# Order of the first loads, no held-back loads, and a new engine order in a one-core pre-norm block

## The chip, the cores and the metric

The kernel runs on one core of one Trainium2 chip. The metric is the device time of one execution in microseconds (us). Three executions of the kernel before gave 197.2, 198.14 and 198.29 us; the median is 198.14 us.

One further execution was taken by the hardware profiler. All rows of the profile in this document count their time from the first instruction of that execution.

## What is computed

The input is x of 2048 rows by 512 columns in bf16. The reference, cut to what matters:

```python
h  = x + _A_ref(_layernorm(x), A_wqkv, A_wo)
h2 = h + _B_ref(_layernorm(h), B_W_gate, B_W_up, B_W_down)

# _A_ref: 32 heads of 16; each position sees 8 positions, 2 apart
qkv = x @ wqkv
idx = pos[:, None] - (jnp.arange(8) * 2)[None, :]
logits = einsum("bhsd,bhswd->bhsw", q, k[idx]) * 16 ** -0.5   # idx < 0 masked
attn = softmax(logits)
o = einsum("bhsw,bhswd->bhsd", attn, v[idx])
return o @ wo

# _B_ref
gate, up = x @ W_gate, x @ W_up          # 512 -> 1376
return (relu(gate) * up) @ W_down        # 1376 -> 512
```

Attention reaches back 14 positions only, so it is made of elementwise products on VectorE, with small matmuls that sum over the 16 entries of a head. The large matmuls are the projections to q, k and v, the output projection, and the gated MLP.

## The kernel before

**Chunks.** The 2048 rows are four chunks of 512, and a chunk is four blocks of 128 rows. A step is named here as in the code, with the chunk behind a slash: `qkv5/1` is the sixth projection of chunk 1. The steps that matter below are these.

- `xst`, `xag` (lines 465 to 472): mean and variance of one block on DVE, from the block of x that a DMA has brought into `x_sm`. `xrl`, `xre` (491, 492): the reciprocal root on ACT, by Ln and Exp.
- `xxn` (495 to 510): the normalised block into a `row` tile, on ACT for chunks 1 and 3 (line 498, with `xnb` on DVE ahead of it), on DVE for chunks 0 and 2 (line 501).
- `xtp` with `xte` or `xtv` (523 to 548): transpose of the block on PE and its copy out of PSUM into a `quad` tile, by ACT or, for block 1 of chunk 0, by DVE at line 544. Chunk 3 has `xtd` (518 to 521) in place of it: a DMA transpose from `row` to `quad` on SP's queue, four of them.
- `qkv0` to `qkv11` (565 to 598): twelve projections of four matmuls each, q and k in turn (0 to 7), then v (8 to 11), each moved out of PSUM by ACT at line 579 (`qe`). In chunk 0 the first six are split into three parts, `qka`, `qkb`, `qkc`; `qka` needs the first two blocks of x and the first two pieces of the q, k weights alone.
- `pr0`, `pr1` (605 to 644): products of q and shifted k on DVE, for the near and the far four of the eight positions. In chunk 0 each is four half-size products (line 634); elsewhere two of full size (line 619). `sc` (625) sums them on PE, `ex` (683) is the exponential on ACT, `mk` (686) the mask of chunk 0 on DVE.
- `bd0S`, `bd1S` (741 to 747): four DMAs each on SP's queue, which spread one `ex` tile over the partitions of a `big` tile.
- `mu` (line 775, or 790 in two halves `mu..a` and `mu..c` for chunk 0): attention weights times shifted v on DVE. `ta` (818): the sum of the two halves of that product by an accumulating DMA of 512 KB, issued from POOL. `tree`, `om` (778, 782, 812): the rest of the sum on DVE, and in chunk 0 the division.
- `wo` (854, 857), `rs`, `hnm`, `hsq`, `hxn`, `htp` or `htd`: output projection, residual and second layer norm. `mm` (927, 894), `ue`, `ge`, `gu`: gate and up projections. `dn` (977), `o`, `os`: down projection, residual and store.
- `lg` (834 to 839): a copy on POOL that makes the loads of the up and down weights, `ldu` and `ldd`, wait for the last `tree` or `om` step with t = 3 of chunk 0.

**Order.** The program is not written in this order. Every step is added to a plan with its engine, a modelled duration, what it depends on and what buffers it takes. The list `RANK` at the top has one number for each step in the order of adding; each engine executes its steps in rising rank. So `RANK` fixes the sequence of PE, DVE, ACT, SP and POOL, and the engines work through it strictly in that sequence. The modelled durations and the due times `XT`, `WT` of the loads only say which of several equal buffers a step gets and how the sequences are merged into one program.

**First loads.** `setup()` (312 to 346) issues the loads of the first microseconds. SP's and ACT's queues take in turn a block of x of chunk 0 (128 KB) and a piece of the q, k weights (256 KB), lines 315 to 319. Behind them on SP's queue come the four blocks of chunk 1 (335), the v weights (337), chunks 2 and 3 of x (340), the output weights (342) and the gate weights. Three tiny copies on POOL, lines 333, 336 and 338, hold these loads back: each reads a tile that an earlier load fills and writes into the tile of the next load, so that next load waits for the earlier one to land.

**Filling.** `warm` (416 to 422) is 56 matmuls of 128 columns on a zeroed tile. `fill` (424 to 430) adds `NFILL` more behind the transposes of blocks 0 and 1.

Of the kernel before, what the change touches and what calls it, by code (L numbers as in the profile page):

```python
# [12 lines left out]
ACT = mybir.ActivationFunctionType  # L13
ALU = mybir.AluOpType
# [188 lines left out]
def kernel(  # L203
# [11 lines left out]
    nc = tc.nc  # L215
    Bsz, S, D = A_x.shape
# [3 lines left out]
    NT = D // P  # L220
# [7 lines left out]
    PRD = ()  # L228
    ODA = (0, 1)
# [9 lines left out]
    BPC = CS // P  # L239
# [72 lines left out]
    def setup():  # L312

        w3_r = A_wqkv.rearrange("(dt p) f -> p dt f", p=P)
        for i in range(2):
            for n, q in enumerate((nc.sync, nc.scalar)):
                j = 2 * i + n
                q.dma_start(x_sm[:, j:j + 1, :], x_rows[:, j:j + 1, :])
                q.dma_start(wqk_sb[:, j:j + 1, :], w3_r[:, j:j + 1, 0:2 * D])  # L319
# [13 lines left out]
        nc.gpsimd.tensor_copy(out=x_sm[0:1, BPC:2 * BPC, 0:1], in_=x_sm[0:1, 3, 0:BPC])  # L333
        for j in range(BPC, 2 * BPC):
            nc.sync.dma_start(x_sm[:, j:j + 1, :], x_rows[:, j:j + 1, :])
        nc.gpsimd.tensor_copy(out=wv_sb[0:1, 0, 0:1], in_=wqk_sb[0:1, 3, 0:1])
        nc.sync.dma_start(wv_sb[:], w3_r[:, :, 2 * D:3 * D])
        nc.gpsimd.tensor_copy(out=x_sm[0:1, 2 * BPC, 0:1], in_=x_sm[0:1, 2 * BPC - 1, 0:1])
# [35 lines left out]
    NWARM, NFILL = 56, (13, 10, 0)  # L374
    NHALF = 6
    XT = (3.55, 3.4, 6.1, 5.85, 9.0, 9.3, 9.6, 10.0, 15.2, 16.75)
    WT = (7.7, 7.7, 5.6, 12.05, 18.0, 24.95, 21.45, 28.8)
# [21 lines left out]
    MM, TP = 0.2165, 0.057  # L399
    SW = 0.21  # L400
    PEL = 0.22
    A5, A10, AX, AS = 0.485, 0.91, 0.75, 0.21
# [151 lines left out]
    for tk in range(NCK):  # L554
# [50 lines left out]
        for hf in range(2):  # L605
            sc, ex = Buf(at_s), Buf(ex_s)
            scd, prd = [], []
            for t in range(0, NT, 2):
# [13 lines left out]
                def f_sc(t=t, sc=sc, pb=pb):  # L622
                    for u in range(2):
                        for g in range(4):
                            nc.tensor.matmul(sc.t[g * HB:(g + 1) * HB, :], lhsT=sel[:],  # L625
                                             rhs=pb.t[:, 4 * u + g, :], start=(t + u == 0),
                                             stop=(t + u == NT - 1), tile_position=(0, g * HB))
# [13 lines left out]
                else:  # L641
                    a = add(("pr%d" % hf, tk), "DVE", D40, f_pr, [d[k] for k in (t, t + 1) for d in (qd, kd, kp)],
                            apr, take=[pb], use=[qT], lat=DL)
                    prd.append((a, pb, f_sc))
# [29 lines left out]
            elif tk in MERGE:  # L674
                scd = [add(("sc%d" % hf, tk), "PE", 4 * MM + SW, lambda p=prd: [f() for _, _, f in p],
# [173 lines left out]
        for j in range(BPC):  # L849
# [20 lines left out]
            if tk in RPE:  # L870
                a = add(("rs%d" % j, tk), "ACT", 0.57, f_rs, [a], base + 50, take=[sm], use=[od], lat=AL)
            else:
                a = add(("rs%d" % j, tk), "DVE", 0.63, f_rs, [a], base + 50, take=[sm], use=[od], lat=DL)
# [190 lines left out]
```

## Time and profile before

| what | value |
|---|---|
| median of three executions | 198.14 us (197.2 to 198.29) |
| span of the profiled execution | 199.0 us |
| PE busy in it | 189.6 us, 1120 matmuls |
| DVE, ACT, POOL busy | 147.9, 116.7, 17.7 us |
| mean granted TensorE clock | 0.991 |
| first projection matmul starts | 8.32 us |
| longest wait of PE | 3.06 us, ends at 37.20 us |
| last matmul ends | about 195.4 us |

How to read the rows that follow. A row of the timeline has the start, the time, the engine (PEld is the weight load of TensorE, SPq the queue that SP issues from), the line of the kernel, the operation, the tile that it writes and those that it reads, the shape, and how often in a row. Behind it, in brackets, is the time that the engine had been idle and what ended that. A row of a table of windows has the stretch, its length, the busy time of PE, PEld, DVE, ACT and POOL, then the granted TensorE clock, the busy share of the 16 DMA engines and the rate in GB/s. One operation's busy time contains some latency, so where several follow each other, the distance from start to start is what one costs.

### The profile page before, as it was taken

The numbers are of one execution on the slowest core, as the hardware profiler recorded it, in microseconds if no ns is written. First come the engines' busy times: TensorE is split into PE (matmuls) and PEld (weight loads), VectorE is DVE, ScalarE is ACT, GpSimd is POOL, SyncE is SP. The second block draws the span as 40 slices with busy tenths as digits, with TensorE's granted clock in tenths as the row PEclk, the third lists the DMA queues.
The fourth block names the chain that finished last, engine by engine and source line by source line (L and its number), as shares of the span: only waits on it lengthen the run. The fifth ranks groups of instructions, "written<-read, shape, count | busy, mean of one in ns | idle before, by whom it ended". The sixth has DMA issues, their size and how long they took to land.

```text
span 199.0 us, 3083 instructions
## 1 busy us (share of the span) xinstructions
PE 189.6 (95%) x1120; PEld 98.5 (50%) x1139; DVE 147.9 (74%) x239; ACT 116.7 (59%) x241; POOL 17.7 (9%) x35
## 2 busy tenths in 40 slices
PE   8899998599999999999999999999999999999992
PEld 8895455245445534554444445544454544455451
DVE  6889999969969999999998769999954311214322
ACT  3579999326779676775536659606458725146300
POOL 3000002520000003300024010010010010000000
PEclk9999999879999999999999999999999999999999
DMA  6889386999600535967379973360030454000303
GB/s 207 231 274 381 96 183 126 190 187 350 217 0 0 137 78 105 190 127 160 80 146 174 188 174 65 65 120 3 0 53 8 103 178 110 0 0 0 109 6 126
DMA packets 25070, 24.61 MB, mean 124 GB/s; under 512 B 11136, under 2 KB 21344, under 8 KB 25056
## 3 DMA queue, kind: packets, MB, share of 16 engines
q1 hardware_dynamic: 22032, 16.23, 29.7%
q0 software_dynamic: 2304, 7.34, 20.2%
q10 hardware_dynamic: 720, 0.85, 1.2%
q8 instruction: 9, 0.15, 0.3%
q14 instruction: 5, 0.04, 0.1%
HBM read 8.42 MB, written 2.10 MB: 53 GB/s over the span
## 4 chain that ended last, share of the span: by engine, by line
PE 90%; DMA 5%; ACT 1%; issue 1%; DVE 1%; ACTq 0%
PE bank L927 34%; PE bank L571 20%; PE bank L977 19%; PE bank L854 7%; PE bank L625 4%; PE bank L894 3%; DMA quad<-row 3%; DMA x_sm<-in_A_x_dram 2%; PE bank L530 1%; ACT quad L579 1%; PE bank L857 0%; PE bank L700 0%; DVE st L466 0%; ACT lnd L706 0%; ACTq L319 0%
## 5 line engine op out<-in xcount | busy, mean ns | idle before, releaser
L927 PE MATMUL bank<-quad,wgu_sb 128*128 128x512 bf16 x311 | 72.0, 379 | 0.4
L927 PEld LDWEIGHTS <-wgu_sb 128*128 128x128 bf16 x320 | 31.0, 98 | 36.5 <-issue 0.8
L977 PE MATMUL bank<-wd_sb,gT 128*128 128x512 bf16 (+2 forms) x185 | 40.4, 367 | 0.2
L571 PE MATMUL bank<-quad,wqk_sb 128*128 128x512 bf16 (+1 forms) x149 | 31.2, 358 | 3.5 <-DMA quad<-row 3.1
L931 ACT CAST up_sb<-bank 128x512 bf16<-128x512 f32 x40 | 22.8, 589 | 19.5 <-PE bank L927 15.9
L934 ACT ACTIVATE gr<-bank 128x512 bf16<-128x512 f32 x40 | 23.3, 601 | 17.6 <-PE bank L927 10.9
L619 DVE TENSOR_TENSOR big<-quad,kT 128x4096 bf16<-128x4096 bf16 x12 | 27.2, 2284 | 2.4 <-ACT quad L579 2.2
L977 PEld LDWEIGHTS <-gT 128*128 128x128 bf16 (+1 forms) x187 | 18.1, 98 | 19.7 <-issue 0.4
L775 DVE TENSOR_TENSOR big<-big,vT 128x4096 bf16<-128x4096 bf16 x12 | 27.1, 2284 | 0.4 <-issue 0.2
L571 PEld LDWEIGHTS <-wqk_sb 128*128 128x128 bf16 x152 | 17.0, 115 | 15.1 <-issue 6.0
L955 DVE TENSOR_TENSOR gT<-gr,up_sb 128x1024 bf16<-128x1024 bf16 x20 | 13.7, 686 | 12.4 <-ACT up_sb L931 7.9
L990 DVE TENSOR_TENSOR row<-x_sm,bank 128x512 bf16<-128x512 bf16 (+1 forms) x9 | 5.5, 625 | 17.0 <-PE bank L977 17.0
L818 POOL DMA_DIRECT2D big<-big x12 | 10.5, 872 | 85.4 <-DVE big L775 59.8
L778 DVE TENSOR_TENSOR big<-big 128x1024 bf16<-128x1024 bf16 (+2 forms) x24 | 16.7, 728 | 0.8 <-DMA big<-big 0.8
L571 PE MATMUL bank<-quad,wv_sb 128*128 128x512 bf16 x61 | 15.7, 380 | 0.3 <-issue 0.2
L854 PE MATMUL bank<-wo_sb,quad 128*128 128x512 bf16 x62 | 14.9, 379 | 0.1
L579 ACT CAST vT<-bank 128x512 bf16<-128x512 f32 x16 | 9.0, 603 | 7.4 <-PE bank L571 7.4
L455 ACT ACTIVATE row<-x_sm,mv 128x512 bf16<-128x512 bf16 x12 | 8.5, 713 | 5.4 <-DVE mv L447 5.3
L466 DVE BATCH_NORM_STATS2 st<-x_sm 128x6 f32<-128x512 bf16 x16 | 10.3, 675 | 0.8 <-DMA x_sm<-in_A_x_dram 0.8
L546 ACT COPY quad<-bank 128x1024 bf16<-128x1024 bf16 (+1 forms) x10 | 8.5, 890 | 4.0 <-PE bank L530 4.0
L501 DVE TENSOR_SCALAR row<-x_sm,mv,rs 128x512 bf16<-128x512 bf16 x24 | 8.9, 406 | 2.5 <-ACT rs L483 2.5
L579 ACT CAST quad<-bank 128x512 bf16<-128x512 f32 x16 | 9.3, 593 | 2.3 <-PE bank L571 2.1
(77 smaller groups left out, 167.0 us busy)
## 6 DMA issues: line engine op xcount, KB each, us to landing
big<-big POOLq DMA_DIRECT2D x12, 512.0 KB, 5.4
big<-ex SPq DMA_DIRECT2D x32, 128.0 KB, 3.1
wgu_sb<-in_B_W_gate_dram SPq DMA_DIRECT2D x2, 688.0 KB, 9.2
wgu_sb<-in_B_W_up_dram SPq DMA_DIRECT2D x2, 688.0 KB, 6.0
wd_sb<-in_B_W_down_dram SPq DMA_DIRECT2D x2, 640.0 KB, 8.2
x_sm<-in_A_x_dram SPq DMA_DIRECT2D x2, 512.0 KB, 6.5
x_sm<-up_sb POOLq DMA_DIRECT2D x4, 256.0 KB, 3.4
out_dram<-x_sm SPq DMA_DIRECT2D x4, 256.0 KB, 3.1
```

Of the source, the lines that this page charges most:

```text
L571: nc.tensor.matmul(mm.t[:, lo:hi], lhsT=wv_sb[:, dt, t:D:NT] if c == 2 else wqk_sb[:, dt, c * D + t:(c + 1) * D:NT], rhs=xnT.t[:, dt, lo:h ...
L579: nc.scalar.copy(out=o, in_=mm.t[:])
L619: V.tensor_tensor(out=pb.t[:].rearrange("p (t w) s -> p t w s", t=2), in0=q4, in1=k4, op=ALU.mult)
L775: V.tensor_tensor(out=mt.t[:], in0=ab.t[:], in1=v8, op=ALU.mult)
L778: V.tensor_tensor(out=mt.t[:, 0:n, :], in0=mt.t[:, 0:n, :], in1=mt.t[:, n:2 * n, :], op=ALU.add)
L818: nc.gpsimd.dma_start(mt.t[:, 0:4, :], mt.t[:, 4:8, :], accum_op=ALU.add)
L854: nc.tensor.matmul(od.t[:], lhsT=OT.t[:, t, j * P:(j + 1) * P], rhs=wo_sb[:, t, :], start=(t == 0), stop=(t == NT - 1 and tk not in RPE))
L927: nc.tensor.matmul(mm.t[:fs, lo:hi], lhsT=wgu_sb[:, dt, g, ft * P: ft * P + fs], rhs=hnT.t[:, dt, lo:hi], start=(dt == 0), stop=(dt == NT ...
L931: nc.scalar.copy(out=ub.t[:fs, i, :], in_=um.t[:fs, :])
L934: nc.scalar.activation(out=gr.t[:fs, i, :], in_=gm.t[:fs, :], func=ACT.Relu)
L955: V.tensor_tensor(out=gt.t[:fs, 0:n, :], in0=gr.t[:fs, 0:n, :], in1=ub.t[:fs, 0:n, :], op=ALU.mult)
L977: nc.tensor.matmul(od.t[:, c0:c1], lhsT=gts[ft].t[:fs, ft % 2, j * P:(j + 1) * P], rhs=wd_sb[:fs, ft, c0:c1], start=(ft == 0), stop=(ft == ...
```

## The change

Four things are changed. (1) In `setup()`, SP's and ACT's queues first take two blocks of x of chunk 0 each, and then two pieces of the q, k weights each. (2) The three copies on POOL that held the later loads back are gone; the loads follow at once on SP's queue. (3) `NFILL` is 8 and 6 where it was 13 and 10. (4) `RANK` is another list, and the model's durations and due times are other numbers.

`PRH` is an empty table, so the code that it guards adds no step, and the `start` and `stop` marks of line 625 come out as before. Number and kind of all steps are as before, apart from the three copies and nine filling matmuls.

```diff
 RANK = [
     0, 1, 2, 3, 4, 5, 6, 7, 8, 9, 10, 11, 12, 13, 14, 15, 16, 17, 18, 19,
-    20, 22, 23, 25, 28, 30, 31, 21, 24, 26, 27, 32, 35, 38, 40, 34, 39, 41, 43, 46,
+    21, 24, 26, 29, 33, 37, 36, 20, 22, 25, 27, 31, 35, 40, 39, 23, 28, 30, 32, 42,
...
+    PRH = {}
...
-        for i in range(2):
+        for i in (0, 2):
             for n, q in enumerate((nc.sync, nc.scalar)):
-                j = 2 * i + n
-                q.dma_start(x_sm[:, j:j + 1, :], x_rows[:, j:j + 1, :])
-                q.dma_start(wqk_sb[:, j:j + 1, :], w3_r[:, j:j + 1, 0:2 * D])
+                q.dma_start(x_sm[:, i + n:i + n + 1, :], x_rows[:, i + n:i + n + 1, :])
+        for i in (0, 2):
+            for n, q in enumerate((nc.sync, nc.scalar)):
+                q.dma_start(wqk_sb[:, i + n:i + n + 1, :], w3_r[:, i + n:i + n + 1, 0:2 * D])
...
-        nc.gpsimd.tensor_copy(out=x_sm[0:1, BPC:2 * BPC, 0:1], in_=x_sm[0:1, 3, 0:BPC])
         for j in range(BPC, 2 * BPC):
             nc.sync.dma_start(x_sm[:, j:j + 1, :], x_rows[:, j:j + 1, :])
-        nc.gpsimd.tensor_copy(out=wv_sb[0:1, 0, 0:1], in_=wqk_sb[0:1, 3, 0:1])
         nc.sync.dma_start(wv_sb[:], w3_r[:, :, 2 * D:3 * D])
-        nc.gpsimd.tensor_copy(out=x_sm[0:1, 2 * BPC, 0:1], in_=x_sm[0:1, 2 * BPC - 1, 0:1])
         for tk in range(2, NCK):
...
-    NWARM, NFILL = 56, (13, 10, 0)
+    NWARM, NFILL = 56, (8, 6, 0)
...
-    MM, TP = 0.2165, 0.057
-    SW = 0.21
+    MM, TP = 0.216, 0.056
+    SW = 0.115
```

Sorted by rank, the steps around the places that are discussed below stand so. Letters a and c mark halves, and the chunk is the number behind the slash.

```text
DVE to xtv1, before:  xst0 xag0 xst1 xag1 xxn0 xst3 xxn1 xag3 xst2 xag2 xtv1 (/0)
DVE to xtv1, after:   xst0 xst1 xag0 xag1 xst2 xag2 xxn0 xxn1 xst3 xag3 xtv1 (/0)

DVE, before:  mk0/0 xag/3 x3  xst/2 x2 xnb/3 xst/2 x2  mu3c  xag/2 x4  mu0c mu3a  xxn/2 x2  mu1a
              xxn/2 x2  mu1c mu2c mu2a mu0a  tree3 pr1/1 tree3 tree1 om3 tree1 om1
              pr0/1 pr0/1 tree2 tree0 tree2 tree0 om2 om0  pr1/1
DVE, after:   mk1/0 xag/3 x3  xst/2 x2 xnb/3 xst/2  mu2a  xst/2 xag/2 x4  mu1a xxn/2 mu2c
              xxn/2 x2  mu1c xxn/2 mu3a mu0a mu0c mu3c  tree2 pr0/1 tree2 tree1 om2 tree1
              pr1/1 om1 tree0 tree3 tree0 tree3 om0 om3  pr1/1 pr0/1

ACT, before:  xrl/3 xre/3 xxn/3 xxn/3 qe8/1 xxn/3 xxn/3 xrl/2 qe7/1 xre/2 qe0/1 qe4/1 dl/0 qe11/1
ACT, after:   xrl/3 xre/3 qe11/0 xxn/3 xxn/3 xxn/3 qe11/1 xrl/2 xre/2 qe4/1 xxn/3 qe8/1 qe5/1 qe6/1 qe7/1 xte/2 qe1/1 xte/2

PE, before:   qkv6/1 xtp/2 qkv3/1 xtp/2 x3 | qkv1/3 qkv5/3 qkv6/3 qkv3/3 qkv11/3 qkv3/2 qkv0/2 qkv4/3
              qkv7/3 qkv8/3 qkv1/2 qkv5/2 qkv2/2 qkv6/2 qkv7/2 qkv4/2 qkv11/2 sc0/1 wo0/0
PE, after:    qkv10/1 xtp/2 x3 qkv3/1 den/0 xtp/2 | qkv10/3 qkv6/3 qkv1/2 qkv5/3 qkv8/3 qkv10/2 qkv6/2
              qkv7/2 qkv4/2 qkv3/2 qkv1/3 qkv0/2 qkv9/2 qkv5/2 qkv4/3 qkv11/3 wo3/0

SP, both:     two groups of bd/0 (before bd1S bd0S, after bd0S bd1S), xtd/3 x4, ldu x2, ldd x2, ...
POOL, before: ta3/0 ta1/0 ta2/0 ta0/0 lg      POOL, after: ta2/0 ta1/0 ta0/0 ta3/0 lg
```

The bar in PE's rows marks the first projection that needs the normalised rows of chunk 3. Later, the `wo` steps of chunk 1 stand behind the same set of PE steps as before; on DVE, the last `tree` step of chunk 1 has one full-size product (`pr1/3`) fewer ahead of it, and one `am` and one short `gu` step more.

More of the change, by code (lines that the diff above doesn't have):

```diff
@@ L373 @@
     TDD, TDL = 1.25, 1.5
-    NWARM, NFILL = 56, (13, 10, 0)
+    NWARM, NFILL = 56, (8, 6, 0)
     NHALF = 6
-    XT = (3.55, 3.4, 6.1, 5.85, 9.0, 9.3, 9.6, 10.0, 15.2, 16.75)
-    WT = (7.7, 7.7, 5.6, 12.05, 18.0, 24.95, 21.45, 28.8)
+    XT = (3.47, 3.64, 4.35, 4.5, 7.9, 8.2, 8.5, 8.8, 13.2, 14.7)
+    WT = (7.2, 7.2, 5.6, 12.0, 16.0, 24.95, 19.7, 28.8)
     DMAT = (('h',2,0),('h',2,2),('h',3,0),('h',3,2),('h',1,0),('x',3,0),('x',3,2))
@@ L396 @@
     LNA = ((0, 1, 0, 1), (0, 0, 0, 0))
-    MM, TP = 0.2165, 0.057
-    SW = 0.21
+    MM, TP = 0.216, 0.056
+    SW = 0.115
     PEL = 0.22
-    A5, A10, AX, AS = 0.485, 0.91, 0.75, 0.21
+    A5, A10, AX, AS = 0.48, 0.905, 0.72, 0.21
     AL = 0.13
@@ L620, in f_pr, with f_sc @@
                                     in0=q4, in1=k4, op=ALU.mult)
-                def f_sc(t=t, sc=sc, pb=pb):
-                    for u in range(2):
+                hs = PRH.get((tk, hf, t))
+                def f_sc(t=t, sc=sc, pb=pb, hs=hs):
+                    for u in range(1 if hs else 2):
                         for g in range(4):
@@ L626, in f_sc @@
                                              rhs=pb.t[:, 4 * u + g, :], start=(t + u == 0),
-                                             stop=(t + u == NT - 1), tile_position=(0, g * HB))
+                                             stop=(t == NT - 2 and bool(u or hs)), tile_position=(0, g * HB))
                 if tk in PRS:
@@ L643, with f_ph @@
                             apr, take=[pb], use=[qT], lat=DL)
+                    if hs == "D":
+                        def f_ph(pb=pb):
+                            nc.gpsimd.dma_start(pb.t[:, 0:4, :], pb.t[:, 4:8, :], accum_op=ALU.add)
+                        a = add(("ph%d" % hf, tk), "POOL", 1.0, f_ph, [a], apr, use=[pb], lat=1.1, dq=(0.75, 2.74))
+                    elif hs:
+                        def f_ph(pb=pb):
+                            V.tensor_tensor(out=pb.t[:, 0:4, :], in0=pb.t[:, 0:4, :], in1=pb.t[:, 4:8, :], op=ALU.add)
+                        a = add(("ph%d" % hf, tk), "DVE", D20, f_ph, [a], apr, use=[pb], lat=DL)
                     prd.append((a, pb, f_sc))
@@ L674 @@
             elif tk in MERGE:
-                scd = [add(("sc%d" % hf, tk), "PE", 4 * MM + SW, lambda p=prd: [f() for _, _, f in p],
+                scd = [add(("sc%d" % hf, tk), "PE", (4 - sum((tk, hf, t) in PRH for t in (0, 2))) * MM + SW, lambda p=prd: [f() for _, _, f in p],
                            [a for a, _, _ in prd], apr, take=[sc], use=[b for _, b, _ in prd], lat=PEL)]
@@ L870 @@
             if tk in RPE:
-                a = add(("rs%d" % j, tk), "ACT", 0.57, f_rs, [a], base + 50, take=[sm], use=[od], lat=AL)
+                a = add(("rs%d" % j, tk), "ACT", 0.575, f_rs, [a], base + 50, take=[sm], use=[od], lat=AL)
             else:
-                a = add(("rs%d" % j, tk), "DVE", 0.63, f_rs, [a], base + 50, take=[sm], use=[od], lat=DL)
+                a = add(("rs%d" % j, tk), "DVE", 0.73, f_rs, [a], base + 50, take=[sm], use=[od], lat=DL)
             hd.append((a, od))
```

72 rows, old and new, of the table RANK are left out of this document.

## The prediction

> **What bounds the kernel now.** I read the busy times and slices first, then the chain of waits and PE's own waits, then the timeline around the one long wait.
>
> ```profile
> span 199.0 us, 3083 instructions
> PE 189.6 (95%) x1120; PEld 98.5 (50%) x1139; DVE 147.9 (74%) x239; ACT 116.7 (59%) x241; POOL 17.7 (9%) x35
> PEclk9999999879999999999999999999999999999999
> PE 90%; DMA 5%; ACT 1%; issue 1%; DVE 1%; ACTq 0%
> PE bank L571 <- DMA quad<-row: 3.1, 1, 3.1
> ```
>
> PE is busy for 95% of the span and is 90% of the chain. Its work hardly changes, so only its gaps can be won: the start, one wait of 3.1 us, and a dip of the granted clock in slices 8 and 9. The dip follows the wait:
>
> ```profile
> 31.79 1.22 SPq L519 DMA_TRANSPOSE quad<-row  x1
> 31.64 1.01 POOL L818 DMA_DIRECT2D big<-big  x1 [21.61 <-PE bank L571]
> 33.30 0.84 PE L530 MATMUL bank<-identity,row 128*128 128x128 bf16 x12
> 37.20 5.09 PE L571 MATMUL bank<-quad,wqk_sb 128*128 128x512 bf16 x15 [3.06 <-DMA quad<-row]
> DMA to landing us min/median/max: 2.4/2.6/5.3
> 32.00:33.00 1.00, 1.00 (x9) 0.66 (x8) 1.00 (x2) 1.00 (x3) 0.64 (x1) 1.00 0.36 72
> 33.00:34.00 1.00, 1.00 (x15) 0.76 (x12) 1.00 (x3) 1.00 (x3) 0.00 (x0) 1.00 1.06 196
> 37.20:42.30 5.10, 5.09 (x15) 2.12 (x17) 5.10 (x7) 0.00 (x0) 2.82 (x3) 0.67 1.03 192
> ```
>
> The landing row is that of chunk 3's four DMA transposes. The last is issued at 31.79; at the minimum of 2.4 us it would be in at 34.2, just as PE, done at 34.14 (33.30 + 0.84), wants it. It takes 5.3 us, to 37.1. The row that stands beside it is POOL's first accumulate, issued 0.15 us earlier; the DMA share jumps from 0.36 to 1.06 at 33.0, 1.4 us after that issue. So 1.2 us of the transpose ran beside the accumulate, and it came 2.9 us late. After the wait PE runs 5.1 us at a clock of 0.67, which loses 5.1 x 0.33 = 1.7 us. Wait and clock cost 4.8 us.
>
> **The start.** These rows say what sets the first projection:
>
> ```profile
> 3.50 0.69 DVE L466 BATCH_NORM_STATS2 st<-x_sm 128x6 f32<-128x512 bf16 x1 [0.30 <-DMA x_sm<-in_A_x_dram]
> 5.98 0.69 DVE L466 BATCH_NORM_STATS2 st<-x_sm 128x6 f32<-128x512 bf16 x1 [0.48 <-DMA x_sm<-in_A_x_dram]
> 7.79 0.39 DVE L544 COPY quad<-bank 128x512 bf16<-128x512 bf16 x1
> 8.32 0.60 PE L571 MATMUL bank<-quad,wqk_sb 128*128 128x256 bf16 x4 [0.33 <-ACT rs L479]
> 7.67 0.18 POOL L336 COPY wv_sb<-wqk_sb 1x1 bf16<-1x1 bf16 x1 [1.47 <-DMA wqk_sb<-in_A_wqkv_dram]
> 3.50:4.00 0.50, 0.50 (x8) 0.50 (x6) 0.50 (x1) 0.42 (x1) 0.00 (x0) 1.00 1.06 410
> 7.00:7.50 0.50, 0.46 (x8) 0.46 (x9) 0.50 (x2) 0.36 (x2) 0.00 (x0) 1.00 0.15 47
> ```
>
> DVE's copy at 7.79 is the last thing that the projection at 8.32 needs. The same ten DVE steps stand ahead of it in both orders, and the only wait among them that the loads cause is 0.48 us for a block of x at 5.98. That block had 1 MB of first loads up to its end and now has 0.5 MB; at about 0.4 MB per us (410 GB/s) it comes some 1.3 us sooner, at 4.7, and the wait goes. I take -0.4 us, between 0 (DVE's waits on ACT grow instead) and -0.5. The first two weight pieces get 0.25 MB more ahead of them, 0.65 us; even if they had landed as late as block x3, that is 6.6, and the projection wants them at 7.9. The last two keep 1.5 MB; POOL's wait shows them landed at 7.67, wanted after 8.5. Nine filling matmuls fewer only empty a gap in which PE waits for DVE's copy, so nothing; if that cover were gone they would be a gain of under 0.7 us.
>
> The three copies that held loads back left the DMA engines nearly empty for a microsecond (share 0.15 at 7.0). Filling it brings x of chunk 1 and the v weights a microsecond or so sooner, which is worth nothing: PE has no wait for weights, and DVE's two waits for x are the two above. On SP's queue the later issues move up with it; its next consumers, the `bd` groups, come at 21.63 and find the queue long empty.
>
> **The wait at 37.20.** It ends with the fourth transpose, so three times must be worked out: when that is issued, when the first accumulate starts, and when PE asks.
>
> ```profile
> 21.63 6.04 SPq L743 DMA_DIRECT2D big<-ex  x8
> 27.77 2.62 SPq L519 DMA_TRANSPOSE quad<-row  x2
> 27.18 1.23 DVE L790 TENSOR_TENSOR big<-big,vT 128x2048 bf16<-128x2048 bf16 x1 [0.41 <-DMA big<-ex]
> 28.32 0.37 DVE L469 BATCH_NORM_AGGREGATE mv<-st 128x2 f32<-128x6 f32 x4
> 29.81 1.23 DVE L790 TENSOR_TENSOR big<-big,vT 128x2048 bf16<-128x2048 bf16 x1
> 30.95 0.73 DVE L501 TENSOR_SCALAR row<-x_sm,mv,rs 128x512 bf16<-128x512 bf16 x2
> 33.38 4.62 DVE L790 TENSOR_TENSOR big<-big,vT 128x2048 bf16<-128x2048 bf16 x4
> 25.49 1.28 DVE L466 BATCH_NORM_STATS2 st<-x_sm 128x6 f32<-128x512 bf16 x2
> 27.50 1.53 ACT L498 ACTIVATE row<-x_sm,nb,rs 128x512 bf16<-128x512 bf16 x2
> 28.92 0.29 ACT L479 ACTIVATE rs<-mv,eps_t 128x4 f32<-128x4 f32 x1
> ```
>
> SP issues eight broadcasts and then four transposes without a pause. The broadcasts start behind the mask step on DVE, which in both orders follows the eight score products; of the 0.4 us of the start I let 0.3 through. So broadcasts at 21.3, first transpose 27.45, fourth three issues of 1.31 later (2.62 / 2), at 31.4. DVE's first half-size product then starts at 26.9 for 27.18.
>
> A new wait enters here. Before, the four rows of chunk 3 were done by 29.0 (27.50 + 1.53). Now the fourth stands on ACT behind `xrl/2`, `xre/2` and `qe4/1`, and `xrl/2` waits for DVE's `xag/2`, which moved behind a half-size product: 26.9 + 1.14 + 0.63 (`xst`) + 0.3 (`xag`) = 29.0. Add 0.6 for the two small ACT steps, 0.55 for the evacuation and 0.75 for the row: 30.9. It is ready 0.5 us before SP reaches it, so the wait costs nothing as long as that margin holds; behind it queue ACT's evacuations of chunk 1, and PE with eight banks behind them. For a PE wait on banks I allow 0 to 0.8 us and take 0.4, as PE showed none before but ACT now pauses about a microsecond.
>
> POOL's first accumulate now follows `mu2c`: 29.0 + 1.14 (`mu1a`) + 0.35 (`xxn/2`) + 1.14 = 31.6. Before, the product of 29.81 ended at 31.04 and POOL issued at 31.64; the same 0.6 gives 32.2, and traffic from 33.6. The transpose, issued at 31.4 and 2.4 to 2.6 us long, is in at 33.8 to 34.0: 0.2 to 0.4 us beside the accumulate where it was 1.2. In proportion to the 2.9 us for 1.2, that delays it by 0.5 to 1.0 us; with no proportion (it has nearly finished) by nothing. The Trainium skill (DMA: Bandwidth & Descriptors, Queues, rings and completion order) says that each DMA engine takes turns between its queues packet by packet; an estimate by that page would stretch the shared 0.4 us to 0.8 at most, and 1.2 us to 2.4. The trace shows more, 2.9 us on top of 1.2, so here the measurement decides and the larger delay is kept as a bound.
>
> PE asks at 34.14 - 0.4 + 0.4 = 34.1. I take the wait's end at 34.3, with 33.8 and 35.0 as bounds: **2.9 us earlier than 37.20**, and that includes the start. PE then idles for some tenths, against 3.06 us, so the clock should stay full: **-1.7 us**. On the other side of PE, two projections of chunk 3 (1.7 us) cover the copies that chunk 2 still needs.
>
> **What is late next.** PE comes 4.6 us sooner to steps that DVE feeds.
>
> ```profile
> 38.52 2.28 DVE L619 TENSOR_TENSOR big<-quad,kT 128x4096 bf16<-128x4096 bf16 x1
> 40.72 1.01 DVE L778 TENSOR_TENSOR big<-big 128x512 bf16<-128x512 bf16 x2
> 45.07 4.49 DVE L619 TENSOR_TENSOR big<-quad,kT 128x4096 bf16<-128x4096 bf16 x2 [2.20 <-ACT quad L579]
> 49.48 1.96 DVE L778 TENSOR_TENSOR big<-big 128x1024 bf16<-128x1024 bf16 x4
> 51.36 0.75 DVE L782 TENSOR_TENSOR quad<-big,rec 128x512 bf16<-128x512 bf16 x2
> 56.65 0.15 DVE L447 TENSOR_SCALAR mv<-sm 128x1 f32<-128x1 f32 x1 [2.08 <-ACT x_sm L863]
> 60.22 2.59 PE bank L571 x12
> 90.50 0.42 DVE L812 TENSOR_TENSOR quad<-big 128x512 bf16<-128x512 bf16 x1
> 91.16 3.45 PE bank L854 x16
> ```
>
> First, `wo3/0`. PE needs 16 projections of 4 x 0.216 (2.59 / 12): 34.3 + 13.8 = 48.1. DVE ends its half-size products at 26.9 + 8 x 1.14 + 0.63 + 0.3 + 1.3 = 38.3; then come two products of 2.2, two early trees of 2.75 together and the four last trees with two divisions, 2.6 (49.48 to 52.1): 48.1. They meet, so a wait of 0 to 1.1 us; the last accumulate, issued at 38.9, is the one that could add it.
>
> Second, `wo` of chunk 1: DVE was done at 90.9, PE came at 91.16. DVE drops one product of 2.2 and takes up 0.7 of short steps ahead of that point, and its idle 2.20 and 2.08 us, which were waits for a late PE, can close. That is 1.5 to 5.8 us sooner against PE's 4.2, so a wait of 0 to 2 us. For both places, and the short ones between, I take **+0.4**; from chunk 2 on the trace has idle DVE time, and the end of the kernel keeps its shape.
>
> Sum: -2.9 - 1.7 + 0.4 = **-4.2 us**, span 194.8. The profiled execution's own span of 199.0 lies 0.9 above the median of the runs, so the time is 198.14 - 4.2 = **193.9 us**.
>
> **Rivals.** (a) **The collision returns.** The margin of a microsecond between transpose and accumulate is the difference of two sums of five terms. If SP's issues run 0.5 us later and POOL 0.5 earlier, the transpose again takes 5.3 us: 31.4 + 5.3 = 36.7. Gain 0.5 of the wait, the clock as before: 197.6; with the clock saved at a shorter idle of 2.6 us, 196. The Trainium skill (TensorE: Matmul & The Clock Gate, What's actually happening) gives about 3.4 us of idle as the window that drops the clock to half; by that the 2.6 us would be spared, and 196 be the time. The row shows the drop after 3.06 us, so the trace does not settle it.
>
> (b) **Slower: the fourth row of chunk 3 comes late on ACT.** It hangs on broadcast, half-size product, `xag/2`, Ln, Exp, an evacuation, and only then the row, where before it hung on none of these. Each microsecond that this chain is late moves transpose and accumulate together, so the two collide in any case: issue + 5.3. From an issue at 32.5 (1.1 us later than worked out) the wait ends later than 37.8 and the kernel loses over 0.5%; at 33.0 it ends at 38.3, 1.1 us later than before, with the clock dropped as before and 0.4 behind it: 199.6. For it: ACT had 15.05 of 16.10 us busy just there. Against it: 0.5 us of margin by the sum.
>
> ```profile
> 15.70:31.80 16.10, 15.87 (x108) 8.24 (x109) 15.68 (x31) 15.05 (x29) 0.17 (x1) 1.00 0.66 196
> ```
>
> (c) **The blocks come no sooner**, because both queues fill the engines already (share 1.06). Then the start keeps its 8.32 and everything behind it 0.3: 194.3, inside the forecast's own range.
>
> **How the numbers follow.** Forecast with (c): chance 0.58, own range 192.3 (no wait behind 33.8, all of the clock) to 195.6 (wait's end at 35.0, 1.4 us of new waits). Rival (a) 0.20, half of it on each side of 0.5%, which is about what a measurement of this kernel tells from no change (1.0 us). Rival (b) 0.22, of which 0.04 stays within 0.5%: its margin is half a microsecond behind seven steps in a row. So faster 0.68, same 0.14, slower 0.18. The range runs from 192.3 to 197.8: it takes in (a) and leaves out (b).
>
> **What would show it.** The first `qka` near 7.9 for 8.32, with no DVE wait for x behind 3.5; broadcasts at 21.3; the fourth transpose landing in under 3.2 us; PE's wait there under 1 us and a granted clock of 1.00 from 37 to 42; `wo` of chunk 0 at 48 and of chunk 1 at 87. I am wrong if a transpose of chunk 3 again takes 5 us, or if PE's list of waits has a new one of over 2 us.

## The result, and the profile after

| | before | after |
|---|---|---|
| executions, median (lowest to highest) | 198.13 us of 4 (197.2 to 198.29) | 201.27 us of 4 (200.47 to 201.94) |
| ratio, 95% interval | | 1.0162 (1.0128 to 1.0195) |
| spans of the executions | 199.0 (the one profile of before) | 198.3, 198.6, 199.6, 199.8 |

The kernel became 1.6% slower; the forecast was 193.9 us, 2.1% faster, and its range ended at 197.8. Here and below, a ratio is taken from fast runs alone, those within 1.5% of the fastest of the same kernel, while medians and counts are of all executions. These are the lines of the page of the changed kernel that answer to the first ones of before:

```profile
span 199.6 us, 3062 instructions
PE 191.9 (96%) x1130; PEld 99.0 (50%) x1130; DVE 147.4 (74%) x239; ACT 115.8 (58%) x241; POOL 21.0 (11%) x32
PEclk9999999999999999996999999999999999999999
PE 56%; DVE 16%; DMA 15%; issue 6%; SPq 3%; POOL 1%; DVEq 0%; POOLq 0%
```

The dip of the granted clock has gone from slices 8 and 9 and stands in slice 19 instead, at 90 to 95 us. DMA, 5% of the chain of waits before, is 15% now. PE's own waits, and the timeline of the start and around chunk 3's transposes, in the changed kernel:

```profile
PE bank L865 <- DVE quad L823: 2.3, 2, 2.1
PE bank L570 <- ACT quad L578: 0.6, 1, 0.6
PE bank L570 <- DMA wqk_sb<-in_A_wqkv_dram: 0.4, 1, 0.4
```

```profile
7.84 0.70 PE L570 MATMUL bank<-quad,wqk_sb 128*128 128x256 bf16 x4
9.16 0.47 PE L570 MATMUL bank<-quad,wqk_sb 128*128 128x256 bf16 x2 [0.41 <-DMA wqk_sb<-in_A_wqkv_dram]
10.20 1.29 DVE L465 BATCH_NORM_STATS2 st<-x_sm 128x6 f32<-128x512 bf16 x2 [1.78 <-DMA x_sm<-in_A_x_dram]
22.26 6.07 SPq L754 DMA_DIRECT2D big<-ex  x8
...
31.81 0.81 ACT L497 ACTIVATE row<-x_sm,nb,rs 128x512 bf16<-128x512 bf16 x1
31.96 1.02 PE L570 MATMUL bank<-quad,wv_sb 128*128 128x512 bf16 x4 [0.59 <-ACT quad L578]
...
32.65 1.19 SPq L518 DMA_TRANSPOSE quad<-row  x1
33.75 1.01 POOL L829 DMA_DIRECT2D big<-big  x1 [31.31 <-DVE row L500]
33.82 0.72 PE L529 MATMUL bank<-identity,row 128*128 128x128 bf16 x8 [0.29 <-DVE row L500]
```

The first projection starts at 7.84, as forecast, and the 3.06 us wait at chunk 3's transposes is gone. But SP's first broadcasts start at 22.26, where they stood at 21.63 before and were forecast at 21.3. New is a wait of 2.10 us at `wo` of chunk 1. The next rows show where that one comes from. Line 738 is the step `am`, which scales chunk 2's `ex` tiles on DVE; the broadcasts `bd0S/2`, `bd1S/2` on SP (line 754) read them. Line 829 is the accumulate `ta` of chunk 1, and line 789 is the first `tree` step, which needs it.

```profile
81.35 0.86 POOL L829 DMA_DIRECT2D big<-big  x1 [1.34 <-DVE big L786]
82.18 0.42 DVE L738 TENSOR_TENSOR ex<-ex,rec 128x512 bf16<-128x512 bf16 x1
82.62 7.74 SPq L754 DMA_DIRECT2D big<-ex  x8
87.89 0.38 PE L865 MATMUL bank<-wo_sb,quad 128*128 128x512 bf16 x1
89.16 0.69 DVE L789 TENSOR_TENSOR big<-big 128x1024 bf16<-128x1024 bf16 x1 [2.55 <-DMA big<-big]
90.37 2.18 PE L865 MATMUL bank<-wo_sb,quad 128*128 128x512 bf16 x7 [2.10 <-DVE quad L823]
```

The table of windows of the same kernel, with the columns as before, gives the clock behind the wait, and the piece of the chain of waits (start, time, what) gives the transfer:

```profile
88.00:90.00 2.00, 0.27 (x2) 0.00 (x0) 0.81 (x2) 0.00 (x0) 0.00 (x0) 1.00 0.80 225
90.00:92.00 2.00, 1.63 (x7) 0.74 (x8) 1.88 (x5) 0.00 (x0) 0.00 (x0) 0.85 0.89 215
92.00:94.00 2.00, 2.00 (x6) 0.68 (x5) 0.76 (x3) 0.61 (x1) 0.00 (x0) 0.50 0.88 59
94.00:96.00 2.00, 2.00 (x9) 0.84 (x8) 1.38 (x5) 1.11 (x5) 0.00 (x0) 0.79 0.01 1
```

```profile
81.35 7.79 DMA big<-big
```

Read from the bottom up. The fourth accumulate of chunk 1 is issued at 81.35 and takes 7.79 us, to 89.14. DVE, idle for 2.55 us, then starts the `tree` step at 89.16, and PE follows at 90.37. From there PE works 6 us at a mean clock of 0.85, 0.50 and 0.79, which loses 2 x (0.15 + 0.50 + 0.21) = 1.7 us. Only 1.3 us behind the accumulate, SP began to issue the eight broadcasts of chunk 2. In the profile of before the same accumulate and the same broadcasts are 5.3 us apart, and the accumulate landed in 5.7 us:

```profile
83.00 0.86 POOL L818 DMA_DIRECT2D big<-big  x1 [1.95 <-DVE big L775]
88.33 6.00 SPq L743 DMA_DIRECT2D big<-ex  x8
```

The long accumulate could have been read there all the same, one chunk later: chunk 2's last accumulate was issued at 108.47, chunk 3's broadcasts from 109.24 on, and it is the slowest in the landing row of all twelve accumulates of that profile. PE did not wait for it.

```profile
DMA to landing us min/median/max: 4.5/5.4/7.6
```

Against the spans of before, whose median over ten executions is 195.9 us (the first experiment below), the two executions at full clock are 2.4 and 2.7 us longer, the other two, with a mean clock of 0.991, 3.7 and 3.9.

### The profile page after: what moved, and what is told of

It reads as the page before. It is cut to its first block, busy times and chain, and to the rows that moved or that the text cites. A ratio compares the mean times of both kernels' runs of the same rounds, so it can differ in the third digit from the quotient of the medians.

```text
span 199.6 us, 3062 instructions
## 1 busy us (share of the span) xinstructions
PE 191.9 (96%) x1130; PEld 99.0 (50%) x1130; DVE 147.4 (74%) x239; ACT 115.8 (58%) x241; POOL 21.0 (11%) x32
## 4 chain that ended last, share of the span: by engine, by line
PE 56%; DVE 16%; DMA 15%; issue 6%; SPq 3%; POOL 1%; DVEq 0%; POOLq 0%
PE bank L938 19%; PE bank L988 14%; PE bank L570 11%; PE bank L865 8%; DMA big<-big 8%; DVE big L635 4%; DMA x_sm<-in_A_x_dram 4%; DVE big L786 4%; SPq L754 3%; DMA big<-ex 3%; DVE big L618 2%; PE bank L905 2%; DVE big L801 2%; DVE st L465 2%; PE bank L626 1%
## 5 line engine op out<-in xcount | busy, mean ns | idle before, releaser
L938 PEld LDWEIGHTS <-wgu_sb 128*128 128x128 bf16 x320 | 30.9, 98 | 37.0 <-issue 1.7
L988 PE MATMUL bank<-wd_sb,gT 128*128 128x512 bf16 (+3 forms) x187 | 40.0, 366 | 0.0
L570 PE MATMUL bank<-quad,wqk_sb 128*128 128x512 bf16 (+1 forms) x152 | 30.2, 346 | 0.4 <-DMA wqk_sb<-in_A_wqkv_dram 0.4
L865 PE MATMUL bank<-wo_sb,quad 128*128 128x512 bf16 x64 | 16.8, 411 | 2.3 <-DVE quad L823 2.3
L865 PEld LDWEIGHTS <-quad 128*128 128x128 bf16 x64 | 6.5, 104 | 11.6 <-DVE quad L823 3.2
L876 DVE SCALAR_TENSOR_TENSOR x_sm<-x_sm,bank 128x512 bf16<-128x512 bf16 x12 | 8.2, 687 | 4.3 <-PE bank L865 4.2
L801 DVE TENSOR_TENSOR big<-big,vT 128x2048 bf16<-128x2048 bf16 x8 | 9.5, 1219 | 2.0 <-DMA big<-ex 2.0
```

The costliest lines, as they stand in the source:

```text
L570: nc.tensor.matmul(mm.t[:, lo:hi], lhsT=wv_sb[:, dt, t:D:NT] if c == 2 else wqk_sb[:, dt, c * D + t:(c + 1) * D:NT], rhs=xnT.t[:, dt, lo:h ...
L801: V.tensor_tensor(out=mt.t[:, 4 * hf:4 * hf + 4, :], in0=ab.t[:, 4 * hf:4 * hf + 4, :], in1=v4, op=ALU.mult)
L865: nc.tensor.matmul(od.t[:], lhsT=OT.t[:, t, j * P:(j + 1) * P], rhs=wo_sb[:, t, :], start=(t == 0), stop=(t == NT - 1 and tk not in RPE))
L938: nc.tensor.matmul(mm.t[:fs, lo:hi], lhsT=wgu_sb[:, dt, g, ft * P: ft * P + fs], rhs=hnT.t[:, dt, lo:hi], start=(dt == 0), stop=(dt == NT ...
L988: nc.tensor.matmul(od.t[:, c0:c1], lhsT=gts[ft].t[:fs, ft % 2, j * P:(j + 1) * P], rhs=wd_sb[:fs, ft, c0:c1], start=(ft == 0), stop=(ft == ...
```

## The experiments

The theories are named by letters in the expectations. R: the profile of before that the forecast was read from was not typical, so the 4.8 us of wait and clock were not there to be won. L: the loads that are no longer held back crowd each other and cost time. O: the loss lies in the new order. B: within O, chunk 2's broadcasts share the DMA engines with chunk 1's last accumulate. Q, against B: the accumulates only queue behind one another, whatever SP issues.

All ratios are against the kernel before in the same series on the same chip; the interval is 95%.

| run | first loads | order | median us (executions) | ratio | profiled span |
|---|---|---|---|---|---|
| `base_again` | before | before | 197.73 (10) | 0.9996 (0.9964 to 1.0027) | 196.6 |
| `loads_only` | new, not held | before | 196.96 (10) | 0.9949 (0.9929 to 0.9969) | 194.7 |
| `loads_again` | new, not held | before | 197.40 (12) | 0.9987 (0.9962 to 1.0012) | 194.7 |
| `x_first_old_order` | new, held | before | 197.16 (10) | 0.9996 (0.9978 to 1.0014) | 195.1 |
| `order_only` | before | new | 201.06 (4) | 1.0128 (1.0055 to 1.0201) | 198.9 |
| `x_first_held` | new, held | new | 199.22 (10) | 1.0065 (1.0027 to 1.0103) | 197.6 |
| `late_bd2` | new, not held | new, 1 move | 199.74 (4) | 1.0123 (1.0090 to 1.0156) | 197.9 |
| `late_bd2_held` | new, held | new, 1 move | 199.56 (4) | 1.0110 (1.0053 to 1.0167) | 197.7 |
| `late_bd2_row4` | new, held | new, 2 moves | 198.98 (5) | 1.0080 (1.0051 to 1.0109) | 196.4 |
| `gtd_first` | new, held | new, 3 moves | 198.17 (10) | 1.0024 (0.9994 to 1.0054) | 195.8 |
| `gtd_first_nohold` | new, not held | new, 3 moves | 198.34 (10) | 1.0004 (0.9967 to 1.0042) | 196.0 |

**The kernel before, once more.** No edit.

> The kernel before, unchanged. In the changed kernel's runs the time lies 2.2 us above the span. Theory R (the profiled execution of before was not a typical one): the timed runs of before have spans near 196, and in another profile the wait of 3.06 us behind chunk 3's DMA transposes is shorter than 1 us or absent, with a granted clock of 1.00. Rival: the wait is in every execution; then the span is near 199 again with the time near 198, or the time of the profiled execution is 201.

It has no long wait. These are its span, the clock, PE's first wait and the landing row of chunk 3's four transposes, which had 5.3 us at its end before:

```profile
span 196.6 us, 3083 instructions
PEclk9999999999999999999999999999999999999999
PE bank L530 <- DVE row L501: 1.8, 3, 1.3
DMA to landing us min/median/max: 2.4/2.5/2.8
```

And its timeline at the start and around those transposes:

```profile
7.43 0.69 DVE L466 BATCH_NORM_STATS2 st<-x_sm 128x6 f32<-128x512 bf16 x1 [2.03 <-DMA x_sm<-in_A_x_dram]
9.78 0.60 PE L571 MATMUL bank<-quad,wqk_sb 128*128 128x256 bf16 x4 [0.33 <-ACT rs L479]
29.26 5.25 SPq L519 DMA_TRANSPOSE quad<-row  x4
33.94 1.01 POOL L818 DMA_DIRECT2D big<-big  x1 [22.35 <-DVE row L501]
36.28 3.40 PE L571 MATMUL bank<-quad,wqk_sb 128*128 128x512 bf16 x15
```

Here a block of x came late (DVE waits 2.03 us at 7.43 where it had waited 0.48), everything behind it is 1.5 us later, and yet the span is 2.4 us shorter than the first profile's: the fourth transpose meets no accumulate, and PE has no wait for it. Over the three series 78 executions of this kernel had spans of 194.6 to 197.7 us, and in none was the mean clock below 0.995; the first profile had 199.0 and 0.991. The time of an execution is about 1.8 us above its span. So R holds: the execution that I read was worth about 200.8 us, not 198.1.

**Loads alone, order alone, and the order with held loads.** The first is the kernel before with parts 1 and 2 of the change, `NFILL` as before. The second is the changed kernel with the first loads and the three holding copies as before. The third is the changed kernel with the holding copies put back alone. The new order thus always comes with the new `NFILL` and the model's new numbers.

```diff
-        for i in range(2):
+        for i in (0, 2):
...
-        nc.gpsimd.tensor_copy(out=x_sm[0:1, BPC:2 * BPC, 0:1], in_=x_sm[0:1, 3, 0:BPC])
...
-        nc.gpsimd.tensor_copy(out=wv_sb[0:1, 0, 0:1], in_=wqk_sb[0:1, 3, 0:1])
...
-        nc.gpsimd.tensor_copy(out=x_sm[0:1, 2 * BPC, 0:1], in_=x_sm[0:1, 2 * BPC - 1, 0:1])
```

> The kernel before with the new first loads alone (x blocks first, nothing held back), old engine order. Theory L (the loads that are no longer held back crowd the q, k weights and x of chunk 1): slower than before by 1 to 2 us, x of chunk 1 landing 5 us or more after its issue, DVE waiting over 1 us for it near 9 to 10 us. Theory O (the loss is the new order's): within 0.5 us of before, or faster by up to 0.5.

> The changed kernel with the first loads of before (x and weight pieces in turn, three copies on POOL that hold the later loads back). Theory L: as fast as before or faster, 196 to 198.2. Theory O: near the changed kernel, 200 to 201.5, with PE's wait of about 2 us at the output projection of chunk 1.

> The changed kernel with the three copies on POOL put back, x blocks still first. Theory L in its narrow form (it is the missing holds, not the order of the first eight loads): 1 us or more faster than the changed kernel, the first block of chunk 1 in before 9 us. Theory O: near 201. If the order of the first eight loads matters too, it differs from the kernel with the new order and the old loads by over 0.5 us.

The loads alone gain 0.5% in this series, although x of chunk 1 landed 4.7 to 5.7 us after its issue and DVE waited 1.20 us for it, the signs that L had named. The order alone loses 1.3%, most of it where the clock fell: its one execution at full clock took 198.68 us, 0.4% above before. PE's wait at `wo` of chunk 1 and the windows behind it in the run with the order alone show the same picture as the changed kernel:

```profile
PE bank L867 <- DVE quad L825: 2.4, 2, 2.2
```

```profile
90.00:92.00 2.00, 2.00 (x8) 0.83 (x7) 1.41 (x4) 0.00 (x0) 0.00 (x0) 0.68 1.05 152
92.00:94.00 2.00, 2.00 (x7) 0.61 (x5) 1.06 (x6) 0.81 (x2) 0.00 (x0) 0.50 0.04 4
```

So O holds: the order loses without the new loads. That does not put L out. `x_first_held` has the same wait, 2.08 us, but its clock fell in 2 of 10 executions only (201.70 and 201.79 us), against 2 of 4 of the changed kernel and 3 of 4 of `order_only`. It stands about 2 us below the changed kernel, as L in its narrow form had asked for, and not near 201, as O had. At full clock its median is 198.7 us, against 200.47 and 200.74 of the changed kernel in an earlier series, and PE's waits in the two profiles differ by 0.4 us only. So a part of the changed kernel's loss may lie in the missing holds. The later pairs with and without them do not show it; this stays open.

**Broadcasts of chunk 2 later.** The changed kernel with `am0/2` and `am1/2` moved on DVE behind the last `tree` step of the second half of chunk 1, so that SP issues their broadcasts later; alone, with the loads held, and (last) with the fourth row of chunk 3 moved ahead on ACT, right behind the third.

```diff
+            last = max(o.prio for o in self.ops if o.key == ("tree1", 1))
+            for o in self.ops:
+                if o.key in (("am0", 2), ("am1", 2)):
+                    o.prio = last + 0.25
...
+            rows = sorted((o for o in self.ops if o.key == ("xxn", 3)), key=lambda o: o.prio)
+            rows[3].prio = rows[2].prio + 0.25
```

> The changed kernel with two steps of DVE moved: am0/2 and am1/2, which release chunk 2's eight broadcasts, stand behind the last tree step of chunk 1. Theory B (those broadcasts, issued 0.8 to 1.3 us behind chunk 1's fourth accumulate, share the DMA engines with it, which makes the accumulate 7.8 us long and the output projection of chunk 1 late): the accumulate lands in under 6.5 us, PE's wait of 2.1 us before that projection is under 0.5, the clock stays at 1.00 and the time falls by 2 us or more to under 199.3. Rival Q (the four accumulates queue behind each other, whatever else runs): still over 7 us, still a wait of 2 us, 200.5 to 202.

> The same move in the kernel with the new order and the three holding copies put back (199.22 without the move). Theory B: 197.0 to 197.8, and a smaller spread between executions, since those of 201.7 with a granted clock of 0.991 go. Rival Q: 199 again, same spread.

> The kernel of the run before with one more step moved: on ACT, the fourth normalised row of chunk 3 stands right behind the third, ahead of the steps that wait for chunk 2's statistics. If ACT's pause there is what makes PE wait for a bank near 32 us (0.5 us, and 0.3 us near 33.5), the wait goes and the time falls by 0.3 to 0.8 us more. If the pause is covered, no difference.

In `late_bd2` the broadcasts go out at 88.98. Timeline, and the landing row of the accumulates issued between 76 and 82.2 us (7.8 at its end in the changed kernel):

```profile
81.41 0.86 POOL L833 DMA_DIRECT2D big<-big  x1 [1.34 <-DVE big L790]
87.47 0.69 DVE L793 TENSOR_TENSOR big<-big 128x1024 bf16<-128x1024 bf16 x1 [1.14 <-DMA big<-big]
88.67 3.41 PE L869 MATMUL bank<-wo_sb,quad 128*128 128x512 bf16 x15 [0.64 <-DVE quad L827]
88.98 5.60 SPq L758 DMA_DIRECT2D big<-ex  x8
94.68 1.25 SPq L928 DMA_TRANSPOSE gT<-row  x1
97.73 1.48 PE L992 MATMUL bank<-wd_sb,gT 96*128 96x512 bf16 x6 [1.76 <-DMA gT<-row]
```

```profile
DMA to landing us min/median/max: 5.4/5.5/6.0
```

The accumulate with the same neighbours on POOL takes 6.0 us at most where it took 7.8, and PE's wait shrinks from 2.10 to 0.64 us. In none of the four executions did the clock fall. The other traces agree: with the broadcasts 1.3 us behind it this accumulate took 7.8 to 8.0 us (`order_only`, `x_first_held`), and 6.0 us at most in all five with the broadcasts moved. That is B, and against Q at this place. Accumulates do hold each other up where they are closer: two that POOL issued 0.9 us apart in the kernel before, from 37.41 on, landed in 5.0 and 7.0 us.

But clock apart the time stays: the ratio is 1.0123, and that of the changed kernel's two executions at full clock 1.0125, where B had expected under 199.3 us. A DMA transpose of the down projection's input (`gtd/0`, line 928) now stands in SP's queue behind all eight broadcasts, and PE waits 1.76 us for it at 97.73. The wait has moved by one queue. With the loads held the move gains nothing at all: `late_bd2_held` took 199.56 us for the 199.22 without it (1.0110 and 1.0065), where B had expected 197.8 at most. PE waits 1.9 us for `gtd/0` there, and one of its four executions lost the clock.

With the fourth row ahead as well, ACT's pause shrinks from 2.02 to 0.89 us. This is that pause, first in the changed kernel, then in `late_bd2_row4`:

```profile
30.90 0.30 ACT L478 ACTIVATE rs<-mv,eps_t 128x4 f32<-128x4 f32 x1 [2.02 <-DVE mv L468]
```

```profile
30.13 0.30 ACT L487 ACTIVATE rs<-mv,eps_t 128x4 f32<-128x4 f32 x1 [0.89 <-DVE mv L477]
31.19 1.02 PE L579 MATMUL bank<-quad,wv_sb 128*128 128x512 bf16 x4
33.04 0.72 PE L538 MATMUL bank<-identity,row 128*128 128x128 bf16 x8 [0.60 <-DVE row L509]
96.28 1.69 PE L997 MATMUL bank<-wd_sb,gT 96*128 96x512 bf16 x7 [1.47 <-DMA gT<-row]
```

PE's 0.59 us wait for a bank at 31.96 is not there (31.19, no wait). But its next one, for a row of chunk 2, grows from 0.29 to 0.60 us (33.04), so that PE saves about 0.4 us here against `late_bd2_held`. The profiled span falls by 1.3 us and the median by 0.6; with four and five executions that overlap (198.14 to 200.68 and 198.51 to 199.42 us) this is not clear of their spread. The profile of `order_only` has no wait for a bank at this place, so this part of the loss seems to come only with the new loads.

**x first in the old order, loads held.** The kernel before with part 1 of the change alone.

> The kernel before with the x blocks first, nothing else: the three copies still hold the later loads back, the engine order is the old one. If the gain of the new first loads with the old order (196.96 for 197.89) comes from the x blocks landing sooner, this run has it too, 196.7 to 197.2; if it comes from dropping the holds, this run is near 197.9.

```profile
7.89 0.60 PE L572 MATMUL bank<-quad,wqk_sb 128*128 128x256 bf16 x4
9.52 1.88 DVE L467 BATCH_NORM_STATS2 st<-x_sm 128x6 f32<-128x512 bf16 x3 [1.13 <-DMA x_sm<-in_A_x_dram]
```

The first projection stands at 7.89 in this timeline, as early as in the changed kernel, and the time is that of before in this series, 197.41 us. That 197.16 lies in the range expected for a gain settles nothing, as that range was reckoned from the 197.89 of the series ahead. A new wait of 1.13 us for x of chunk 1 on DVE follows at once. This one gain of the change is real at its place and cannot be seen at the end.

**The transpose of `gtd/0` ahead of the broadcasts.** The two moves and a third: on SP `gtd/0` ahead of chunk 2's broadcasts, with the loads held and not held. And the new loads in the old order once more.

```diff
+            bd = min(o.prio for o in self.ops if o.key in (("bd0S", 2), ("bd1S", 2)))
+            for o in self.ops:
+                if o.key == ("gtd", 0):
+                    o.prio = bd - 0.25
```

> The kernel late_bd2_row4 with one step of SP moved: the DMA transpose gtd/0 ahead of chunk 2's eight broadcasts, behind which it stood 6 us. If the wait of 1.5 to 1.9 us near 97 that came with the moved broadcasts is only that queue, it goes: under 0.4 us, and the time falls by 1.2 to 1.8 us to 197.2 to 197.8, so the new order is level with before. If the new order is slower for a reason that I have not found, it stays over 198.5.

> The same three moves in the changed kernel itself, without the holding copies. If the holds are worth nothing by themselves, within 0.4 us of the run before; if their absence delays weights and chunk 1's x in the new order, 0.5 to 1 us slower than it.

> loads_only once more, with more rounds, as the best version so far: the kernel before with the new first loads. Faster than before by 0.3 to 0.9 us (0.1 to 0.5%); if the 0.9 us of the first time was chance, within 0.2 us.

Timeline of `gtd_first`:

```profile
87.47 3.41 PE L878 MATMUL bank<-wo_sb,quad 128*128 128x512 bf16 x15 [0.59 <-DVE quad L836]
88.38 1.44 SPq L937 DMA_TRANSPOSE gT<-row  x1
89.91 5.09 SPq L767 DMA_DIRECT2D big<-ex  x8
```

The wait for `gtd/0` is gone, the time 0.4 us above what was expected at most. Three moves bring the new order nearly level with the old one: 1.0024 and 1.0004, both intervals across 1. By the medians of all ten executions the second is 1.0033, and with the same loads in the old order (`loads_again`) the time is 0.9 us shorter. So the three queue places together hold most of the order's loss; up to 0.5% may be left, and the order gains nothing. What each move is worth alone is not shown, as each was made on top of the one before. Held and not held loads differ by 0.2 us there, so dropping the holds costs nothing that shows.

`loads_again` gives 0.9987 where `loads_only` gave 0.9949: the new loads in the old order are the fastest variant tried, by 0 to 0.5%. One of its 12 executions took 201.01 us at a span of 199.0 and a clock of 0.991, the very numbers of the first profile of before. So such an execution still happens in the old order. Its own wait was not seen, as it was not the profiled one, and the clock of 0.991 alone does not name the wait: the falls at `wo` of chunk 1 show it too.

## Why the prediction was wrong

**What bounds the kernel: the row was right, its weight was not.** The wait of 3.06 us and the 1.7 us of clock were in the trace. The step that failed is the sentence "The profiled execution's own span of 199.0 lies 0.9 above the median of the runs, so the time is 198.14 - 4.2". A time is not a span: in both kernels it lies 1.8 to 2.2 us above (198.4 for 196.6, 201.8 for 199.6). The profiled execution thus stood for about 200.8 us, 2.7 above the median, and I took away from the median what only that execution had. The forecast itself shows the slip: a span of 194.8 and a time of 193.9, below it. With 2.2 us on top of that span the same sums give 197.0, so 3.1 of the 7.4 us between forecast and result are this step; the other 4.3 are in the span, 194.8 forecast against a median of 199.1. This could be suspected blind: the wait hung on 0.15 us between two issues, and its price was more than the whole spread of the three runs. It was priced as a fixture.

**The start, -0.4: right at its place, not passed on.** 7.84 for 8.32, no DVE wait for x of chunk 0 (in `base_again` the first projection stood at 9.78, so 8.32 was no fixture either). But of the 0.4 us I let 0.3 through to the broadcasts, at 21.3, and they came at 22.26: DVE now waits 1.78 us for x of chunk 1 and has no pause from there to the broadcasts. Part of that comes with the new sequence of the loads alone, as `x_first_old_order` keeps the holds and waits 1.13 us. Of "worth nothing" for the holds, the mechanism was wrong and the verdict about right. Without them the loads land late, in the landing row of chunk 1's four blocks of x:

```profile
DMA to landing us min/median/max: 5.0/5.6/5.8
```

It was 2.1 to 2.4 us before. The weights are late too: PE waits 0.41 us for them at 9.16, DVE 1.78 for x at 10.20. "DVE's two waits for x are the two above" was a fact of the old order, not a bound. In time it shows neither in `loads_again` nor in `gtd_first_nohold`; for the changed kernel it is the question that `x_first_held` leaves open.

**The wait at 37.20: the mechanism was right, the size less than half.** Forecast were a fourth transpose at 31.4 and an accumulate at 32.2; they came at 32.65 and 33.75, 1.3 and 1.6 us late and 1.1 us apart for 0.8. The collision did not return: rival (a) is out, and the landing, 2.7 us at most, and the full clock from 37 to 42 are as I said they would be. Rival (b) had its first half: the fourth row of chunk 3 ended at 32.62 (31.81 + 0.81), not 30.9, because ACT waited 2.02 us for `xag/2`, and the transpose left 0.03 us later. But accumulate and transpose moved together and kept their distance, so it cost PE's wait of 0.59 us on a bank and 0.29 us on a row, not 5.3 us of landing. My 0.4 for this was half of what it took. With the 0.41 us for weights, PE came to chunk 3's projections at 35.89, not at 34.3: the term of -2.9 measures -1.3 against the profile that I read, and -0.4 against `base_again`, where PE came at 36.28.

**What is late next: the second failed step.** "For both places ... I take +0.4." The first place, `wo3/0`, came at 49.71 with no wait. The second had 2.10 us, just beyond the "0 to 2" that I had allowed and past the 2 us that I had named as the sign of being wrong, and then 1.7 us of clock that stood in no term. Only the size seems off, but the reason was missing too: I counted DVE's work ahead of `wo`, and DVE had time enough, it stood idle 2.55 us. What was late was a transfer. I had noted "one `am` ... step more" ahead of that point and not followed it to what it releases: eight broadcasts on SP, 128 KB each, in the shadow of the accumulate that `tree` waits for. Nor did I look for the price of such a meeting, 7.6 us for one accumulate, in the profile of before, where it stood. `late_bd2` shows what it was worth here: 1.46 us of the wait.

**The clock as a cliff.** I argued that tenths of idle would spare the clock, and did not ask what the wait of up to 2 us that I allowed at `wo` would do. In the profiled executions the clock fell behind waits of 2.10 us (the changed kernel) and 2.17 us (`order_only`) and not behind 2.08 us (`x_first_held`). The Trainium skill (TensorE: Matmul & The Clock Gate, What's actually happening) lets the clock fall to half after at least one idle window of about 3.4 us. Here 2.1 us was enough, so the measurement decides. The waits of the other executions were not recorded. Kernels profiled with 2.08 to 2.17 us at that place lost the clock in 7 of 18 executions (the changed kernel 2 of 4, `order_only` 3 of 4, `x_first_held` 2 of 10), those with a longest wait of 1.47 to 1.76 us in none of 9 (`late_bd2_row4`, `late_bd2`), and `late_bd2_held`, at 1.9 us, in 1 of 4. In this kernel the chance of a fall is to be priced from about 2 us on.

**The sum, made again.** Between the two profiles: -1.3 for the -2.9, -1.7 for the clock as forecast, and +2.1 and +1.7 for the +0.4. That is +0.8 us, and the spans differ by 0.6 (199.0 and 199.6). Against the usual execution of before, from the changed kernel's rows: +2.10 (`wo` of chunk 1), +0.59, +0.29 and +0.41, and -0.5 for the start is 2.9 us; the executions at full clock are 2.4 to 2.7 us longer. It is a rough account: the kernel before has small waits of its own that vary, and the rows are those of an execution whose clock fell. The fall of the clock adds 1.3 us by the spans, 1.7 by the windows. One figure of the range does not come out of its terms either: its lower end was put at 192.3, and an end of the wait at 33.8 without new waits gives 193.0.

## What to carry to other kernels

Before a wait in a profile is priced as a gain, compare that execution with the timed ones on the same scale: span plus what lies between span and time in that kernel (1.8 to 2.2 us here), and the clock. A wait that hangs on a tenth of a microsecond between two issues may belong to one execution in many. And when a step is moved, follow it through the queue that it feeds to the transfers that share the engines there; here, broadcasts issued a microsecond behind an accumulate made that accumulate late, and the next transfer in the same queue inherited what the cure saved.

## What the runs showed of the hardware

- **A transpose beside an accumulate has a sharp edge.** Accumulate issued 0.15 us ahead of the fourth transpose (before): the slowest transpose 5.3 us. Issued 0.14 us behind it (`loads_again`, 31.42 and 31.56): 3.2 us. Behind it by 0.45 (`loads_only`), 0.65 (`base_again`), 1.1 us (the changed kernel): 2.8, 2.8, 2.7 us. Three tenths of a microsecond decide over 2 us, in one profile of each.
- **Broadcasts and an accumulate slow each other.** The accumulates of 512 KB of chunk 1 took 4.5 to 6.0 us without broadcasts close behind and 7.8 to 8.0 us with the eight 1.3 us behind; chunk 2's last one took 7.6 us in the kernel before with the eight 0.8 us behind. SP's issue of the eight took 7.74 us in the changed kernel and 5.60 in `late_bd2`.
- **A part of the time lies outside the span.** In the mean 1.83 us in the kernel before and `x_first_old_order`, 1.86 in `late_bd2_held`, 2.0 to 2.2 in the others, over 4 to 12 executions each (78 of the kernel before). Some 0.3 us of the loss is of this kind; what it is stays open.
